# Padding each row of values, keys and output gates from 968 to 1024 words

## The chip, the cores and the metric

The kernel runs on one core of a Trainium2 chip. The metric is device time in microseconds of one execution of the whole program; of several runs the median is taken. All arithmetic is in float32 unless a line says otherwise.

## The reference, cut to what matters

Two layers stand behind each other. The first is a gated recurrence over 768 steps, for 4 batches and 8 heads of width 40:

```python
for t in range(S):
    m_new = np.maximum(f_gate[:, :, t] + m, i_gate[:, :, t])
    f_stab = np.exp(f_gate[:, :, t] + m - m_new)
    i_stab = np.exp(i_gate[:, :, t] - m_new)
    m = m_new
    C = f_stab[..., None, None] * C + i_stab[..., None, None] * np.einsum('bhd,bhe->bhde', vt, kt)
    n = f_stab[..., None] * n + i_stab[..., None] * kt
    h_tilde = np.einsum('bhde,bhe->bhd', C, qt)
    denom = np.maximum(np.abs(np.einsum('bhd,bhd->bh', n, qt)[..., None]), 1.0)
    y[:, :, t] = h_tilde / denom / (1.0 + np.exp(-o_gate[:, :, t]))
```

The second routes each of the 3072 resulting rows (320 wide) to one of 4 groups and in it to one of 4 experts; the chosen expert of 16 computes `relu(x @ w1) @ w2` with 1024 hidden units, and the two gate probabilities scale the row.

## The kernel before, in words

The recurrence is computed in chunks of 128 steps. There are 6 chunks by 4 batches, so 24 units, each with all 8 heads; unit u is chunk u // 4 of batch u % 4. `unit(u)` issues the work of a unit, written out by hand so that neighbouring units overlap: loads for units ahead, scores of unit u + 1, results of unit u, the last scaling and the store of unit u - 1. For the instruction order nothing is planned by the compiler; each engine runs its list as written.

A unit needs three inputs and leaves one output, all moved by DMAs that SyncE (SP) issues on one queue:

- `qk`: keys and queries, transposed, in two DMAs of 40 partitions each, one row of 1024 words to a partition (`load_qk`, lines 157 and 158).
- `nt`: for each of 128 steps a row with 328 words of values (each head's 40 and a one), 320 words of keys and 320 words of output gates, 968 words in all (`load_nt`, line 183). The source is a DRAM array that the host lays out as 24 blocks of 128 rows without gaps. Four tiles take turns.
- `ab`: the decays of the unit's 8 heads, one row of 1024 words that is sent to all 128 partitions (`load_ab`, line 173).
- `x_d`: the unit's 128 result rows of 384 words, stored to DRAM (`store_rows`, line 315), from where the second layer gathers them. In four units a block of 128 rows of zeros is stored too (line 459).

So the queue of SP carries, per unit, in this order: `ab`, `qk`, `qk`, `nt`, `x_d`. Each DMA has one of eight landing counters in turn, and an issue waits until the DMA eight places ahead of it has landed; SP is therefore never more than eight DMAs ahead.

Readers of an `nt` tile are `gate` (ScalarE, tanh of the 320 gate words), `keyw` (GpSimd, keys times decay), `state` and `values` (TensorE, with the values as the moving operand), and `gated` (VectorE, gates times results):

```python
o = st_[u]["nt"][:, NTW:NTW + DM]                      # gate, line 162
t["nt"][:, DM + H:NTW]                                 # keyw, line 220
mm(..., t["kw"][:, j, :], nt[:, j * D1:(j + 1) * D1])  # state, line 257
```

They address words 0 to 967 of a row. `NTW` is 648, the words ahead of the gates.

After the units come the routing, the lists of rows for each expert, and the experts themselves in order of their load; they use neither `nt` nor its array, but their tiles reuse the memory of the units.

Of the kernel before, what the change touches and what calls it, by code (L numbers as in the profile page):

```python
# [7 lines left out]
F32 = mybir.dt.float32  # L8
# [10 lines left out]
P = 128  # L19
B, H, S, D = 4, 8, 768, 40  # L20
NCH = S // P
NU = NCH * B
DM = H * D
# [12 lines left out]
D2 = 2 * D1  # L36
WIN = 64
NTW = 2 * DM + H
CW = 56
NQK = 4  # L40
C_ID, C_LT, C_TIE, C_E, C_P, C_CAP, C_FIRST, C_15E, C_BASE, C_RANK, C_END = (
# [23 lines left out]
def bc(ap, shape):  # L65
    return ap.broadcast_to(list(shape))
# [3 lines left out]
def lstm_moe(ctx: ExitStack, tc: tile.TileContext, gates, qkT, nat, wcat, w1, w2, cst, out):  # L70
# [41 lines left out]
    def att_pool(name, bufs, stack=att, **kw):  # L112
        return stack.enter_context(tc.tile_pool(name=name, bufs=bufs, side="right", **kw))
# [8 lines left out]
    up_ = att_pool("unit", 1, unit_tiles)  # L122
    qkp = [up_.tile([P, 2, 4, P], F32, name=f"qk{i}") for i in range(NQK)]
    Cflat = up_.tile([P, B * 4 * 2 * CW], F32, name="Cflat")
    Cbd = Cflat.rearrange("p (a r e) -> p a r e", r=2, e=CW)[:, :, :, 0:D1]
    abs_ = [up_.tile([P, H, P], F32, name=f"ab{i}") for i in range(4)]
    nts = [up_.tile([P, NTW + DM], F32, name=f"nt{i}") for i in range(4)]
    ps_s = att_pool("ps_s", 3, score_banks, space=PSUM)
    ps_a = att.enter_context(tc.tile_pool(name="ps_a", bufs=1, space=PSUM))
    sums = ps_a.tile([P, 512], F32, name="st")[:, 0:8 * D1].rearrange("p (a r e) -> p a r e", r=2, e=D1)  # L130
# [30 lines left out]
    def gate(u):  # L161
        o = st_[u]["nt"][:, NTW:NTW + DM]
        nc.scalar.activation(o, o, AF.Tanh, scale=0.5)
# [51 lines left out]
    def keyw(u):  # L215
        t = st_[u]
        if u // B < NCH - 1:
            kw = wk.tile([P, H, D], F32, name="kw")
            nc.gpsimd.tensor_tensor(kw.rearrange("p (a r) d -> p a r d", r=2),
                                    t["nt"][:, DM + H:NTW].rearrange("p (a r d) -> p a r d", r=2, d=D),  # L220
                                    bc(t["ab"][:, :, P - 1:].rearrange("p (r a) t -> p a r t", r=2), (P, 4, 2, D)), op=ALU.mult)
# [8 lines left out]
    def carried(u):  # L230
        c, b = divmod(u, B)
        t = st_[u]
        if c > 0:
            acc = acc_of(u)
            for pr in range(4):
                o = (b * 4 + pr) * 2 * CW
                for r in HALVES:
                    mm(acc[r, 2 * pr:2 * pr + 2, 0:D1], t["qk"][:, 1, pr, r],
                       Cflat[:, o:o + 2 * CW].rearrange("p (r e) -> p r e", r=2)[:, :, 0:D1], start=(pr == 0), stop=False,
                       skip_group_check=True)  # L240
# [58 lines left out]
    def gated(u):  # L299
        c, b = divmod(u, B)  # L300
        sr = st_[u]["sr"] = wk.tile([P, H, D], F32, name="sr")
        nc.vector.scalar_tensor_tensor(sr, st_[u]["nt"][:, NTW:NTW + DM].rearrange("p (h d) -> p h d", d=D), 1.0, st_[u]["acc"][:, :, 0:D],
                                       op0=ALU.add, op1=ALU.mult)
# [876 lines left out]
    with tc.manual_schedule():  # L1180
# [131 lines left out]
        for r in range(NEARLY, NE):  # L1312
# [8 lines left out]
            if r + 1 < NE:  # L1321
                first, second = casts(r + 1)
                ahead, k = (1, 1) if CAPS[r] <= P else (1, 2) if CAPS[r] == P + SHORT else (0, 2) if CAPS[r] <= 224 else (0, 4)
# [70 lines left out]
def _lay(inputs):  # L1394
    import numpy as np

    c = np.ascontiguousarray
    q, k, v, o = (inputs[n] for n in ('q', 'k', 'v', 'o_gate'))
    parity = np.r_[0:H:2, 1:H:2]
    gates = c(np.stack([inputs[n][:, parity].reshape(B * H, S) for n in ('f_gate', 'i_gate')], axis=1))  # L1400

    def tr(a):
        return a.reshape(B, H // 2, 2, NCH, P, D).transpose(3, 0, 2, 5, 1, 4).reshape(NCH, B, 2 * D, H // 2, P)

    qkT = c(np.stack([tr(k), tr(q)], axis=3))

    def rows(a):
        return a.reshape(B, H, NCH, P, D).transpose(2, 0, 3, 1, 4)

    vv = np.concatenate([rows(v), np.ones((NCH, B, P, H, 1), v.dtype)], axis=-1)  # L1410
    nat = c(np.concatenate([vv.reshape(NCH, B, P, DM + H)] + [rows(a).reshape(NCH, B, P, DM) for a in (k, o)], axis=-1))
    wg, we = inputs['moe_w_group'], inputs['moe_w_expert']
    wcat = np.concatenate([wg, we.transpose(1, 0, 2).reshape(DM, NE)], axis=1)
    wcat = np.concatenate([wcat, np.zeros((DM, 12), wcat.dtype)], axis=1)
    wcat = np.concatenate([wcat, wcat[2 * P:]], axis=0)
    wcat = c(wcat.reshape(3, P, 32).transpose(1, 0, 2))
    w1 = inputs['moe_w1'].reshape(NE, DM, F)
    w1 = np.concatenate([w1, w1[:, 2 * P:]], axis=1)
    w1 = c(w1.reshape(NE, 3, P, F).transpose(0, 2, 1, 3).reshape(NE, P, 3 * F))
    w2 = c(inputs['moe_w2'].reshape(NE, NF, P, DM).transpose(0, 2, 1, 3).reshape(NE, P, NF * DM))  # L1420
    cst = np.zeros((P, C_END), np.float32)
    cst[:, C_ID:C_ID + P] = np.eye(P)
    cst[:, C_LT:C_LT + P] = np.triu(np.ones((P, P)), 1)
    cst[:, C_TIE:C_TIE + 4] = [4, 3, 2, 1]
    cst[:, C_E:C_E + NE] = np.arange(NE)
    cst[:, C_P] = np.arange(P)
    cst[:, C_CAP:C_CAP + NE] = CAPS
    cst[:, C_RANK:C_RANK + NE] = RANKS
    cst[:, C_FIRST:C_FIRST + NE] = NE - np.arange(NE)
    cst[:, C_15E:C_15E + NE] = NE - 1 - np.arange(NE)  # L1430
    cst[0, C_BASE:C_BASE + NE] = np.arange(NE) * NTOK
    cst[1, C_BASE:C_BASE + NE] = -MID
    return {'gates': gates, 'qkT': qkT, 'nat': nat, 'wcat': wcat, 'w1': w1, 'w2': w2, 'cst': cst}
# [22 lines left out]
```

## Time and profile before

| | |
|---|---|
| median of 3 runs | 381.36 us (378.76, 381.36, 382.41) |
| profiled execution, its own time | 378.54 us |
| its span, first to last instruction | 377.0 us |
| granted clock of TensorE, mean over the span | 0.992 of full speed |
| busy share of the span: TensorE, VectorE, ScalarE, GpSimd | 93%, 78%, 70%, 42% |
| moved by all DMA queues | 89.19 MB, 237 GB/s over the span |

The profile is of one execution. 1.5 us of its time lie outside the span. A DMA is cut into packets, which 16 DMA engines work off; the profile gives for each queue the number of its packets, the bytes, and the time of its packets as a share of 16 engines' time in the stretch. A share over 100% says that packets overlapped or that some ran on past the end of the stretch. Mean time of a packet is that share, times 16, times the length of the stretch, over the number of packets that began in it.

### The profile page before, as it was taken

The numbers are of one execution on the slowest core, as the hardware profiler recorded it, in microseconds if no ns is written. First come the engines' busy times: TensorE is split into PE (matmuls) and PEld (weight loads), VectorE is DVE, ScalarE is ACT, GpSimd is POOL, SyncE is SP. The second block draws the span as 40 slices with busy tenths as digits, with TensorE's granted clock in tenths as the row PEclk, the third lists the DMA queues.
The fourth block names the chain that finished last, engine by engine and source line by source line (L and its number), as shares of the span: only waits on it lengthen the run. The fifth ranks groups of instructions, "written<-read, shape, count | busy, mean of one in ns | idle before, by whom it ended". The sixth has DMA issues, their size and how long they took to land.

```text
span 377.0 us, 10237 instructions
## 1 busy us (share of the span) xinstructions
PE 350.5 (93%) x3809; PEld 310.4 (82%) x3809; DVE 295.6 (78%) x716; ACT 264.0 (70%) x656; POOL 157.2 (42%) x180
## 2 busy tenths in 40 slices
PE   8979989899989769999999989999999999999993
PEld 5747778787777658789999989979989989979993
DVE  5896786778887764588897887898887888889892
ACT  3579777778676454445785875885886788789691
POOL 6586867576745100616322433234322604332131
PEclk9999999999999989999999999999999999999998
DMA  6999999899999790449764866748669759569000
GB/s 187 296 318 323 325 310 323 290 343 343 334 320 316 261 308 5 115 138 343 240 248 158 304 226 198 258 134 285 233 232 285 239 182 314 175 205 287 28 20 15
DMA packets 23572, 89.19 MB, mean 237 GB/s; under 512 B 3904, under 2 KB 7910, under 8 KB 19938
## 3 DMA queue, kind: packets, MB, share of 16 engines
q1 hardware_dynamic: 19442, 76.28, 60.3%
q0 software_dynamic: 3760, 11.87, 10.2%
q8 instruction: 31, 0.51, 0.6%
q10 hardware_dynamic: 320, 0.38, 0.4%
q14 instruction: 19, 0.16, 0.1%
HBM read 78.97 MB, written 10.03 MB: 236 GB/s over the span
## 4 chain that ended last, share of the span: by engine, by line
PE 59%; DMA 16%; issue 9%; DVE 7%; ACT 4%; POOL 3%; POOLq 1%; SPq 0%; DVEq 0%; ACTq 0%
PE psh L770 22%; DMA qk<-in_qkT_dram 10%; DMA x_d<-x 6%; PE po L841 5%; PE po L842 5%; PE po L843 5%; PE po L698 3%; PE sp L207 3%; PE po L814 2%; PE acc L283 2%; ACT ab L198 2%; PE psh L795 2%; DVE w1l L741 1%; PE busy L139 1%; PE lg L350 1%
## 5 line engine op out<-in xcount | busy, mean ns | idle before, releaser
L595 POOL DMA_INDIRECT out_dram<-y,ix x32 | 39.3, 1228 | 105.5 <-ACT y L855 56.5
L770 PE MATMUL psh<-xhl,w1h 128*128 128x256 f32 (+4 forms) x336 | 58.1, 303 | 1.1 <-issue 0.6
L198 ACT ACTIVATE ab<-ab,bcol 128x128 f32<-128x128 f32 x176 | 53.9, 389 | 4.4 <-POOL ab L166 3.8
L841 PE MATMUL po<-w2h,hh 128*128 128x320 f32 (+1 forms) x176 | 55.7, 317 | 0.0
L843 PE MATMUL po<-w2h,hh 128*128 128x320 f32 (+1 forms) x176 | 54.3, 309 | 0.0
L842 PE MATMUL po<-w2l,hh 128*128 128x320 f32 (+1 forms) x176 | 54.3, 309 | 0.0
L770 PEld LDWEIGHTS psh<-xhl,w1h 128*128 128x128 f32 x336 | 49.4, 188 | 3.1 <-issue 1.6
L741 DVE TENSOR_TENSOR w2l<-w2s,w2h 128x640 fp32r<-128x640 f32 x60 | 47.9, 823 | 4.6 <-ACT w2h L737 4.0
L770 PE MATMUL psh<-xhl,wsk 128*128 128x256 f32 (+4 forms) x168 | 47.6, 322 | 0.0
L770 PE MATMUL psh<-xhl,w1l 128*128 128x128 f32 (+6 forms) x256 | 47.5, 267 | 0.0
L591 POOL DMA_INDIRECT xg<-x_d,ix x32 | 32.5, 1017 | 33.9 <-issue 16.5
L741 DVE TENSOR_TENSOR w1l<-w1s,w1h 128x1024 fp32r<-128x1024 f32 x32 | 39.1, 1223 | 7.0 <-ACT w1h L737 6.6
L770 PEld LDWEIGHTS psh<-xhl,w1l 128*128 128x128 f32 x256 | 42.1, 188 | 0.4
L737 ACT CAST w2h<-w2s 128x640 fp32r<-128x640 f32 x60 | 41.7, 724 | 0.1
L207 PE MATMUL sp<-qk 64*128 64x128 f32 x384 | 34.5, 287 | 6.2 <-DMA qk<-in_qkT_dram 4.0
L166 POOL TENSOR_SCALAR_AFFINE_SELECT ab<-ab 128x1024 f32<-128x1024 f32 (+1 forms) x26 | 27.4, 1054 | 26.8 <-DMA ab<-a_d 21.9
L207 PEld LDWEIGHTS sp<-qk 64*128 64x128 f32 x384 | 27.9, 187 | 12.0 <-DVE den L297 3.8
L841 PEld LDWEIGHTS po<-w2h,hh 128*128 128x128 f32 (+1 forms) x176 | 32.6, 185 | 3.4 <-issue 3.1
L212 DVE TENSOR_TENSOR pt<-sp,ab 128x512 f32<-128x512 f32 x48 | 32.0, 683 | 4.1 <-PE sp L207 3.1
L737 ACT CAST w1h<-w1s 128x1024 fp32r<-128x1024 f32 x32 | 33.3, 1044 | 0.0
L843 PEld LDWEIGHTS po<-w2h,hh 128*128 128x128 f32 (+1 forms) x176 | 32.6, 185 | 0.2 <-DVE hh L897 0.2
L842 PEld LDWEIGHTS po<-w2l,hh 128*128 128x128 f32 (+1 forms) x176 | 32.6, 185 | 0.0
(203 smaller groups left out, 738.6 us busy)
## 6 DMA issues: line engine op xcount, KB each, us to landing
w2s<-in_w_dram SPq DMA_DIRECT2D x14, 1280.0 KB
w1s<-in_w_dram SPq DMA_DIRECT2D x12, 1024.0 KB
nt<-in_nat_dram SPq DMA_DIRECT2D x24, 484.0 KB
ab<-a_d SPq DMA_DIRECT2D x22, 512.0 KB
qk<-in_qkT_dram SPq DMA_DIRECT2D x48, 160.0 KB
x_d<-x SPq DMA_DIRECT2D x24, 192.0 KB
w1s<-in_w_dram SPq DMA_DIRECT2D x14, 256.0 KB
w2s<-in_w_dram SPq DMA_DIRECT2D x4, 640.0 KB
```

What stands on the lines that cost most here:

```text
L166: nc.gpsimd.affine_select(out=a, in_=a, pattern=[[0, a.shape[1]], [1, P]], compare_op=ALU.is_ge, fill=fill, base=0, channel_multiplier=-1)
L198: nc.scalar.activation(ab[:, j, :], ab[:, j, :], AF.Exp, bias=bcol[:, c, b * H + j:b * H + j + 1])
L207: mm(t["pm"][hh][:, pr, :], qk[r, 0, pr, :], qk[r, 1, pr, :], start=True, stop=True)
L212: nc.vector.tensor_tensor(pt, t["pm"][hh], t["ab"][:, 4 * hh:4 * hh + 4, :], op=ALU.mult)
L591: return nc.gpsimd.indirect_dma_start(out=o, out_offset=None, in_=src, in_offset=bass.IndirectOffsetOnAxis(ap=idx, axis=0))
L595: return nc.gpsimd.indirect_dma_start(out=out, out_offset=bass.IndirectOffsetOnAxis(ap=idx, axis=0), in_=y, in_offset=None, bounds_check=N ...
L737: nc.scalar.copy(t[names[0]][rows, dst], src[r][rows, s])
L741: nc.vector.tensor_tensor(o, src[r][rows, s], h.bitcast(F32), op=ALU.subtract)
L770: mm(ps[:, g, 0:n_], w[:, s], x, start=(part == 0 and n == 0), stop=(part == 1 and n == len(todo[1]) - 1), skip_group_check=True)
L841: mm(po[0:m], hh[:, f, t], w2h[:, s], start=st0, stop=False)
L842: mm(po[0:m], hh[:, f, t], w2l[:, s], start=False, stop=False)
L843: mm(po[0:m], hh[:, f, tl], w2h[:, s], start=False, stop=sp0)
```

## The change

Each row of 968 words is followed by 56 words of zeros, in the DRAM array and in the four tiles. The rows are laid out on the host, outside the measured time. The one DMA that fills a tile moves whole rows, so it carries the zeros too: 512 KB in place of 484 KB. Nothing reads the added words.

```diff
 NTW = 2 * DM + H
+NTR = 1024
...
-    nts = [up_.tile([P, NTW + DM], F32, name=f"nt{i}") for i in range(4)]
+    nts = [up_.tile([P, NTR], F32, name=f"nt{i}") for i in range(4)]
...
-    nat = c(np.concatenate([vv.reshape(NCH, B, P, DM + H)] + [rows(a).reshape(NCH, B, P, DM) for a in (k, o)], axis=-1))
+    nat = np.concatenate([vv.reshape(NCH, B, P, DM + H)] + [rows(a).reshape(NCH, B, P, DM) for a in (k, o)], axis=-1)
+    nat = c(np.concatenate([nat, np.zeros(nat.shape[:3] + (NTR - NTW - DM,), nat.dtype)], axis=-1))
```

`load_nt` is the same line, `nc.sync.dma_start(nt, nat[c, b])`; line numbers after the new constant are one higher. Every engine's list of instructions, with what each waits for, is the same as before but for the shape of these 24 DMAs. A row now begins at a multiple of 4096 bytes in its block where it began at a multiple of 3872. In the on-chip memory the units' tiles lie at the top end of a stack, so those below the four `nt` tiles (`qk`, `ab`, the state) begin 896 bytes lower, and the four `nt` tiles, 4096 bytes apart now, all begin at the same place modulo 256 bytes, where they had four different ones.

## Rows read from the trace of the kernel before

**Rows 1.** Page, part 2: DMA engines in 40 slices of the span, 9.4 us each.

```profile
DMA  6999999899999790449764866748669759569000
```

**Rows 2.** Chain that ended last, 30 to 125 us: shares by line, then two pieces.

```profile
by line: DMA qk<-in_qkT_dram 41.4%; DMA x_d<-x 22.0%; PE sp L207 9.0%; PE acc L283 7.1%; PE acc L238 3.8%; issue 2.9%; PE lg L350 2.9%; PE tp L325 2.0%; DVE pt L212 1.6%; PE tp L489 1.3%; PE st L257 1.1%; PE lg L356 0.8%; POOL x L307 0.8%; 
...
33.67 7.14 DMA qk<-in_qkT_dram
...
104.09 8.54 DMA qk<-in_qkT_dram
```

**Rows 3.** Waits of SP's queue, 33.7 to 112.7 us: total, times, longest.

```profile
SPq L183 <- DMA ab<-a_d: 12.2, 11, 1.7
SPq L157 <- DMA nt<-in_nat_dram: 4.6, 7, 1.4
```

**Rows 4.** Timeline of SP, one unit: start, length, issue.

```profile
45.46 0.35 SPq L183 DMA_DIRECT2D nt<-in_nat_dram  x1
46.13 0.40 SPq L315 DMA_DIRECT2D x_d<-x  x1
47.27 0.33 SPq L173 DMA_DIRECT2D ab<-a_d  x1
47.96 0.31 SPq L157 DMA_DIRECT2D qk<-in_qkT_dram  x1
...
49.96 0.35 SPq L183 DMA_DIRECT2D nt<-in_nat_dram  x1
```

**Rows 5.** Window 33.7 to 112.7 us: busy time of PE, PEld, DVE, ACT, POOL; clock; DMA.

```profile
33.70:112.70 79.00, 71.47 (x1434) 60.46 (x1430) 60.80 (x219) 59.41 (x212) 53.86 (x75) 1.00 0.99 324
```

**Rows 6.** DMA view, 33.7 to 112.7 us: packets, SP's queue, issues with KB each.

```profile
DMA packets 9056, 25.56 MB, mean 324 GB/s; under 512 B 1149, under 2 KB 3702, under 8 KB 9039
...
q1 hardware_dynamic: 9039, 25.33, 97.5%
...
nt<-in_nat_dram SPq DMA_DIRECT2D x16, 484.0 KB
ab<-a_d SPq DMA_DIRECT2D x15, 512.0 KB
qk<-in_qkT_dram SPq DMA_DIRECT2D x32, 160.0 KB
x_d<-x SPq DMA_DIRECT2D x16, 192.0 KB
x_d<-w1s SPq DMA_DIRECT2D x4, 192.0 KB
```

**Rows 7.** DMA view, 7.1 to 7.3 us.

```profile
DMA packets 14, 0.05 MB, mean 271 GB/s; under 512 B 0, under 2 KB 0, under 8 KB 14
...
q1 hardware_dynamic: 14, 0.05, 67.9%
```

**Rows 8.** DMA view, 134.9 to 135.5 us.

```profile
DMA packets 62, 0.25 MB, mean 423 GB/s; under 512 B 0, under 2 KB 0, under 8 KB 62
...
q1 hardware_dynamic: 62, 0.25, 103.1%
```

**Rows 9.** DMA view, 131.7 to 132.1 us.

```profile
DMA packets 96, 0.15 MB, mean 369 GB/s; under 512 B 0, under 2 KB 96, under 8 KB 96
...
q1 hardware_dynamic: 96, 0.15, 102.5%
```

**Rows 10.** DMA view, 182.9 to 183.7 us.

```profile
DMA packets 39, 0.40 MB, mean 499 GB/s; under 512 B 0, under 2 KB 0, under 8 KB 0
...
q1 hardware_dynamic: 39, 0.40, 117.3%
```

**Rows 11.** Tile `nt`, its loads: length of an issue, min/median/max ns, first and last.

```profile
L183 SPq DMA_DIRECT2D nt<-in_nat_dram x24: 351/352/960, 2.8 to 114.9; - x24
```

**Rows 12.** DMA view, 6.3 to 6.5 us.

```profile
DMA packets 15, 0.05 MB, mean 252 GB/s; under 512 B 2, under 2 KB 2, under 8 KB 15
...
q1 hardware_dynamic: 15, 0.05, 110.6%
```

## The prediction

> **What bounds the kernel now.** I first read the page's slices. TensorE is busy nearly throughout, but the DMA engines have a stretch of their own that is full, the slices from about 9 to 122 us, and idle parts only after it [rows 1]. That is the time of the 24 units; the `nt` loads are issued from 2.8 to 114.9 us [rows 11]. The experts behind it cannot feel the change, except that they begin when the units end: what the units lose or gain reaches the end one for one.
>
> Next, the chain that ended last, between 30 and 125 us. Of these 95 us, 41.4% are the wait for a `qk` load and 22.0% for an `x_d` store, together 60.2 us [rows 2]. The pieces are long (7 to 8.5 us each), far longer than a load's own bytes need, because each is a place in a queue. The queue's waits say the same: SP issues an `nt` load and before it has waited 11 times, 12.2 us in all, for an `ab` load to land, and a `qk` load has waited 7 times for an `nt` load [rows 3]. With eight DMAs in flight and five issued per unit, the reader is to see one thing: whichever transfer the chain names, it stands behind all others, `nt` included, and the chain's DMA time grows with the time of the sum.
>
> The windows view settles how full this is. From 33.7 to 112.7 us the DMA engines have a share of 0.99 while TensorE is busy 71.47 of 79.00 us, at a granted clock of 1.00 (the 2.4 GHz level) throughout [rows 5]. So DMA is the bound there, with TensorE 7.5 us behind it. In these 79 us 16 units pass, 4.9 us each; a unit of the timeline has 4.50 us from one `nt` issue to the next [rows 4].
>
> **The change part by part.** Nothing is removed, no wait is added, no step moves on any queue. 24 loads grow from 484 to 512 KB, 28,672 bytes each. The readers address the same words, so no compute instruction changes. An issue costs SP the same: 0.35 us for `nt` with its 968 words, 0.33 us for `ab` with 1024 [rows 4].
>
> *Is a padded row still one packet?* In the stretch, 16 `nt`, 15 `ab`, 32 `qk` and 20 stores [rows 6] make 16 x 128 + 15 x 128 + 32 x 40 + 20 x 128 = 7,808 rows; with the 1,149 packets under 512 bytes that is 8,957, of 9,056 packets counted. If the 4096-byte rows of `ab` and `qk` were cut in two there would be 3,200 more. So a row of 4096 bytes is one packet, and 128 packets per `nt` load stay 128, eight for each of 16 engines in the mean.
>
> *What does a packet cost?* Four short windows in which all packets are of one size give it, undisturbed:
> - 7.1 to 7.3 us: 14 packets, 271 GB/s x 200 ns / 14 = 3,871 bytes each, so `nt` rows; 67.9% x 16 x 200 / 14 = 155.2 ns [rows 7].
> - 134.9 to 135.5 us: 62 packets of 4,094 bytes by the same sum, that is 4096 (a weight load); 159.6 ns [rows 8].
> - 131.7 to 132.1 us: 96 of 1536 bytes, 68.3 ns [rows 9].
> - 182.9 to 183.7 us: 39 of 10240 bytes, 385.0 ns [rows 10].
>
> The last two give a line of (385.0 - 68.3) / 8,704 = 0.0364 ns per byte. A packet is paid by bytes, not by the piece, which excludes a cost of nothing per packet. For 224 bytes more the line says +8.2 ns; the direct comparison of an `nt` row with a 4096-byte row says 159.6 - 155.2 = +4.4 ns, since the `nt` rows stand about 2 ns above the line. These are both ends of the undisturbed price.
>
> The Trainium skill, page "DMA: Bandwidth & Descriptors", section "How a descriptor splits into AXI transactions", has a rule for that difference: reads start at 256-byte boundaries, and a descriptor that starts between two fetches the unused bytes too, in beats of 32 bytes. Rows at a pitch of 3872 start at all eight multiples of 32, and so would cost 121 to 128 beats, 124.5 in the mean, where a padded one costs 128. That is 2.8% more, and the two rows show 4.4 / 155.2 = 2.8%; by bytes alone it would be 5.8%, 9.0 ns. By the rule the sum below would take its lower end, 0.56 us.
>
> *The sum.* In the DMA-bound stretch there are 16 loads, so 16 x 8 = 128 more costly packets on each engine: 128 x 4.4 ns = 0.56 us, or 128 x 8.2 ns = 1.05 us. A third way, by the rate that the crowded queue reaches there: 16 x 28,672 = 459 KB at 25.33 MB / 79 us = 321 GB/s is 1.43 us [rows 6]. Of this, what falls where the chain runs through DMA reaches the end for certain (60.2 us of it, 76% of 79); in the rest the DMA share is nearly as high, so I let it count in full. The other 8 of the 24 loads [rows 11] are issued before 33.7 us, where the chain runs through compute, or after the stretch; their cost is between nothing, while compute covers them, and 8 x 28,672 bytes at the same rate, 0.72 us, if that cover is gone. I take nothing there, and in the stretch the middle between the two undisturbed prices, 0.8 us: the 4096-byte row is the nearest there is to a padded one, but the `nt` row is of 14 packets only. So +0.8 us, with ends at 0.4 (76% of 0.56) and 2.15 (1.43 + 0.72).
>
> Against the profiled execution that is 378.5 + 0.8 = 379.3 us. That execution was 2.8 us under the median of the runs shown, which themselves spread over 3.7 us; the median moves by the same 0.8 us, to 382.2.
>
> **The rivals.** *Hidden.* The queue has slack that the DMA share doesn't show, and the longer packets only fill it. For it: a unit has 16 engines' share of 0.99, but some of a packet's time is waiting for data, not moving. Then nothing moves: 381.4. Against it: the chain's eight long DMA pieces.
>
> *Faster: the odd starts of the rows are what crowds the engines.* In the stretch the queue's packets took 97.5% x 16 x 79 = 1,232 us of engine time [rows 6]. At undisturbed prices they would take 16 x 128 x 155.2 + 15 x 128 x 159.6 + 32 x 40 x 159.6 + 20 x 128 x 68.3 ns = 1,003 us. So 229 us, 14.3 us per engine, are stretching. If rows that begin at 4096-byte steps ended the `nt` rows' part of it, by their share of the 1,003 us (318, or 32%), that gives back 4.5 us less the 0.8: 377.7. If their odd starts delay the neighbours too, more, down to where TensorE becomes the bound, 7.5 us: 373.9. For it: `nt` is the only load whose rows begin at uneven places. Against it: in a quiet moment its packets take what their bytes ask for, so the unevenness costs 2 ns by itself, and engines that crowd each other explain the rest as well.
>
> *Slower: rows in step.* After the change the rows of all 16 engines begin at the same place modulo 4096 bytes, in DRAM, and their tiles at the same place modulo 256 bytes. If that makes them meet at the same part of a memory, their packets would be stretched as the `nt` packets already are in some moments: from 6.3 to 6.5 us, 13 of them with two tiny ones took 110.6% x 16 x 200 / 13, about 270 ns each [rows 12], 115 ns above the quiet price. At 128 packets per engine that is 14.7 us: 396. The point from which it decides is 3.8 us / 128 = 30 ns per packet. Against it: `qk` rows of 4096 bytes without gaps, and `ab`, one row read 128 times, are in step already, and the stretch carries them at 324 GB/s.
>
> The same page, section "Latency and other measured facts", tells of such a loss where rows lie a large power of two apart: half the rate at 4 MiB, nearly none at 512 KiB. No run here has such a pitch; a padded block is 512 KiB as a whole and its rows are 4 KiB apart, so by that page too this rival is unlikely.
>
> **How the numbers follow.** Forecast, +0.4 to +2.15 us: 0.64. Hidden: 0.20. Faster: 0.08, half of it beyond 1%. Slower: 0.08, nearly all beyond 1%. One per cent, 3.8 us, is about what a measurement of this kernel can tell from no change; forecast and hidden both stay inside it, apart from a few hundredths for the spread of the runs. That makes faster 0.06, same 0.83, slower 0.11. The range takes in forecast and hidden (381.4 to 383.5), about 1.5 us of spread between runs on either side, and the weaker half of the faster rival: 379.0 to 385.2.
>
> **What the profile of the changed kernel would show.** The stretch of full DMA with 16 `nt` loads is 0.4 to 1.5 us longer; MB over the whole span rise by 0.69; the packet count stays; a quiet window with padded rows has about 160 ns per packet; the chain still runs through `qk` and `x_d`, with 55 to 65 us of DMA between 30 and 125 us. Hidden: the same stretch as long as before, at 2% more GB/s. Faster: fewer us of engine time for more bytes, a stretch below 77 us, TensorE's share of it up. Slower: a share of SP's queue over 100% at fewer GB/s, and windows with only padded rows near 200 ns or more. What would make the prediction wrong is an effect of where rows lie, of either sign, above 30 ns per packet; the bytes themselves cannot.

## The result, and the profile after

The changed kernel takes 383.19 us (median of 20 runs, 379.11 to 387.85), the kernel before 380.18 us beside it (20 runs, 374.08 to 383.61): +3.0 us by the medians, 0.8%. The ratio is 1.0124 with an interval of 1.0095 to 1.0153, but it leaves out every run that lies 1.5% above the fastest of its kernel, which for before, with one run of 374.08, is 12 of 20, so the medians are the fairer measure. On another occasion the medians were 382.33 and 379.81, +2.5 us, 0.7%, and the ratio 1.0043 (0.9994 to 1.0091). Resampling the runs gives the two differences of medians an error of 0.7 and 1.1 us. So: slower by 0.7 to 0.8% by the medians; the first comparison excludes no change, the second by itself does not.

The page of the changed kernel, of part 2 the DMA share and the bytes over the span, of part 3 SP's queue:

```profile
DMA  7889999999999972257884786659668768558000
...
DMA packets 23572, 89.88 MB, mean 236 GB/s; under 512 B 3904, under 2 KB 7910, under 8 KB 19938
...
q1 hardware_dynamic: 19442, 76.97, 60.5%
```

The bytes rose by the 0.69 MB that were forecast (89.19 before), and q1 has as many packets as that of a kernel with narrow rows (19,442, below): a padded row is still one packet. The full stretch reaches a slice further than in [rows 1].

The experts cannot be where the time went: from the last `x_d` store of the units to the end it is 242.6 us before and 240.8 after. Over all profiles of the two kernels and of the two with 968-word loads and a wider pitch or tile, told of below, this part takes 240.3 to 242.6 us, while the last store is issued at 134.4 to 136.5 us in the four with narrow rows and at 140.1 and 137.6 in the two of the changed kernel. What is longer lies ahead. I take as the stretch the time from the 8th `nt` issue to the 24th, 16 loads. In before these are at 35.37 and 114.85, after at 36.97 and 117.92 us. The windows view of before for this stretch (busy time of TensorE, its weight loads PEld, VectorE, ScalarE, GpSimd, then clock, DMA share, GB/s):

```profile
35.40:114.90 79.50, 72.05 (x1438) 61.18 (x1440) 61.99 (x223) 59.91 (x214) 54.98 (x77) 1.00 0.99 325
```

The same of after:

```profile
37.00:117.90 80.90, 72.20 (x1438) 61.19 (x1434) 62.14 (x225) 59.96 (x214) 55.24 (x77) 1.00 0.98 322
```

The DMA view of after, same stretch, SP's queue and the `nt` loads:

```profile
q1 hardware_dynamic: 9041, 25.84, 96.4%
...
nt<-in_nat_dram SPq DMA_DIRECT2D x16, 512.0 KB
```

The reader is to see that the rate has not risen (325 to 322 GB/s) while TensorE does the same work (72.05 and 72.20 us): the extra bytes are paid in time. The stretch is 1.5 us longer and begins 1.6 us later. Another 2.6 us of this pair lie between the 24th `nt` issue and the last store, 19.6 us before and 22.2 after; but the second profile of the changed kernel has 19.4 there, and the others with narrow rows up to 21.7, so this part is not the change's. The windows view of that second profile:

```profile
37.00:118.20 81.20, 73.89 (x1464) 62.39 (x1460) 62.42 (x226) 60.54 (x216) 55.14 (x77) 1.00 0.98 323
```

Over all profiles the stretch is 79.49, 78.82, 78.09, 80.24 and 79.70 us with narrow rows in it (mean 79.3) and 80.95, 81.15 and 79.92 with 1024-word rows (mean 80.7): +1.4 us, with an error of 0.5 by their spread. The 8th issue comes at 35.9 us in the mean where the first seven loads are narrow (five profiles, 35.37 to 36.66) and at 36.6 where they are wide (four, 36.21 to 37.02): +0.7, error 0.3, where the narrow ones alone spread over 1.3.

The chain of after, 30 to 125 us, answers to [rows 2]:

```profile
by line: DMA qk<-in_qkT_dram 25.8%; DMA x_d<-x 15.8%; PE sp L208 8.0%; DMA ab<-a_d 7.8%; PE acc L284 7.6%; issue 5.0%; PE acc L239 4.3%; ACT ab L199 2.3%; PE tp L326 2.2%; PE tp L490 1.8%; PE st L258 1.5%; POOL xg L592 1.3%; DVE sr L303 1.3
...
37.64 7.84 DMA x_d<-x
45.49 8.54 DMA qk<-in_qkT_dram
...
79.32 7.45 DMA ab<-a_d
86.78 7.53 DMA qk<-in_qkT_dram
```

Long places in the queue again, with `ab` as a third name. The DMA view of after in a quiet window, 7.4 to 7.6 us, where the second `nt` load lands, as in [rows 7]:

```profile
DMA packets 14, 0.06 MB, mean 287 GB/s; under 512 B 0, under 2 KB 0, under 8 KB 14
...
q1 hardware_dynamic: 14, 0.06, 71.5%
```

That is 71.5% x 16 x 200 / 14 = 163.4 ns per packet, 8.2 above the 155.2 of before: the upper of the two undisturbed prices. By the rule of the Trainium skill, page "DMA: Bandwidth & Descriptors", section "How a descriptor splits into AXI transactions", it would by estimate be 2.8% more; this window shows 5.3%. Since 4096-byte rows of other loads took 159.6 ns [rows 8], 14 packets don't decide it. Loads by themselves, further below, show 2.3% and 3.3%, near that estimate, but not the reason that the rule gives: the same 968 words at even starts, by the same estimate 2.8% cheaper than at uneven ones, took 0.7% more in one run and 0.7% less in another.

### The profile page after: what moved, and what is told of

Read it like the earlier page. It is cut to its first block, busy times and chain, and to the rows that moved or that the text cites. A ratio compares the mean times of both kernels' runs of the same rounds, so it can differ in the third digit from the quotient of the medians.

```text
span 380.9 us, 10237 instructions
## 1 busy us (share of the span) xinstructions
PE 352.7 (93%) x3809; PEld 312.5 (82%) x3809; DVE 293.2 (77%) x716; ACT 264.1 (69%) x656; POOL 160.1 (42%) x180
## 2 busy tenths in 40 slices
DMA packets 23572, 89.88 MB, mean 236 GB/s; under 512 B 3904, under 2 KB 7910, under 8 KB 19938
## 3 DMA queue, kind: packets, MB, share of 16 engines
q1 hardware_dynamic: 19442, 76.97, 60.5%
## 4 chain that ended last, share of the span: by engine, by line
PE 49%; DMA 17%; issue 12%; DVE 10%; ACT 5%; POOL 5%; POOLq 1%; ACTq 0%; DVEq 0%; SPq 0%
PE psh L771 19%; DMA qk<-in_qkT_dram 6%; PE po L842 4%; PE po L844 4%; PE po L843 4%; DMA x_d<-x 4%; PE po L699 3%; ACT ab L199 2%; DMA xg<-x_d,ix 2%; PE sp L208 2%; PE po L815 2%; DMA ab<-a_d 2%; PE acc L284 2%; PE psh L796 2%; DVE w1l L742 2%
## 5 line engine op out<-in xcount | busy, mean ns | idle before, releaser
L742 DVE TENSOR_TENSOR w2l<-w2s,w2h 128x640 fp32r<-128x640 f32 x60 | 47.9, 823 | 4.6 <-ACT w2h L738 2.7
L592 POOL DMA_INDIRECT xg<-x_d,ix x32 | 35.5, 1109 | 33.6 <-issue 16.2
```

Of the source, the lines that this page charges most:

```text
L592: return nc.gpsimd.indirect_dma_start(out=o, out_offset=None, in_=src, in_offset=bass.IndirectOffsetOnAxis(ap=idx, axis=0))
L742: nc.vector.tensor_tensor(o, src[r][rows, s], h.bitcast(F32), op=ALU.subtract)
```

## The experiments

**The queue alone, five kinds of rows.** No computing: SP issues only a unit's five DMAs, over and over.

```python
nc.sync.dma_start(abs_[u % 4], <one row of a_d, to 128>)
nc.sync.dma_start(qk[0:D], qkT[c, b, 0:D])
nc.sync.dma_start(qk[64:64 + D], qkT[c, b, D:2 * D])
nc.sync.dma_start(tiles[k][u % 4][:, 0:n], src[c, b, :, 0:n])
nc.sync.dma_start(x_d[u * P:(u + 1) * P, :], x)
```

> No compute: only the units' five DMAs in their order on SP's queue, 24 units at a time, for five forms of the row load, forwards and backwards (A 968 words of rows of 968; B 1024 of 1024; C 968 words of rows of 1024 into a wide tile; D rows of 968 into a wide tile; E 1032 of 1032); behind them each form's 24 loads with nothing between. The output is not computed, zeros are stored. Theory bytes: per unit B is 0.035 to 0.09 us slower than A, C and D equal A, E is B plus at most 0.015 us. Rival place (where padded rows begin costs more than their bytes): C is as slow as B or slower, E is clearly faster than B although longer. Rival clock (TensorE's clock makes the difference, not the queue): B and A differ by no more than 0.09 us per unit, as by bytes, 2.2 us for 24 units.

Per unit, forward and backward turn: 968 words 4.71 and 4.85 us, 1024 words 4.72 and 4.76, 968 at a pitch of 1024 4.74 and 4.91, 968 in a wide tile 5.17 and 4.98, 1032 words 5.17 and 4.98. One kind differs from itself by up to 0.2, more than what was sought. Inconclusive; but a unit in this bare queue takes within some 5% of what it takes in the kernel (79.5 / 16 = 4.97, with four stores of zeros more in it), so the kernel's stretch runs near the queue's own pace.

**The changed kernel once more, its two parts, and wider rows.** The first is unchanged. The second has the padded array and tile, but moves the 968 words alone. The third pads to 1096.

```diff
-        nc.sync.dma_start(nt, nat[c, b])
+        nc.sync.dma_start(nt[:, 0:NTW + DM], nat[c, b, :, 0:NTW + DM])
```
```diff
-NTR = 1024
+NTR = 1096
```

> The changed kernel once more. All theories: 2.3 to 5.0 us slower than before, in the middle 3.7 (the mean of its 20 runs against the 20 of before), so a ratio of 1.006 to 1.013; its profile tells how much the end of the units moves from one execution to the next.

> Rows lie 1024 words apart in DRAM and in the tiles, but only 968 words of each are moved. Theory bytes: as before, ratio 0.997 to 1.003. Rival place: as the changed kernel, ratio 1.006 to 1.013. Rival clock: between them, by how often the clock falls.

> Rows of 1096 words, 128 added where the change adds 56. Theory bytes: 2.3 times what the change costs: by quiet packet prices 1.8 to 3.6 us, by the crowded rate 4.9 us, so a ratio of 1.005 to 1.013; if the 3.7 us of the change are all bytes, 8.5 us, 1.022. Rival place: the rows no longer begin at steps of 4096 bytes, so no more than the bytes' part, at or under the changed kernel. Rival clock: more idle time, more falls, over 1.013.

Measured beside before at 379.81 (29 runs): again 382.33, ratio above; pitch alone 379.85, 1.0006 (0.9967 to 1.0044); 1096 words 382.68, 1.0084 (1.0046 to 1.0122). The windows view of the kernel with the pitch alone:

```profile
36.10:116.40 80.30, 72.09 (x1458) 61.35 (x1454) 61.65 (x226) 60.60 (x215) 55.09 (x77) 1.00 0.98 319
```

Its page, part 3, SP's queue over the whole span:

```profile
q1 hardware_dynamic: 19442, 76.28, 61.3%
```

At 80.2 us the stretch is the longest of the five with narrow rows (78.1 to 80.2), and the bytes are 0.69 MB fewer than after's with as many packets. So where the rows lie costs nothing and gains nothing that could be seen: both rivals of place fall, the faster one and the slower one. What costs is, as far as these runs tell, the words that are moved. 1096 words add 1.57 MB in 24 loads, 2.3 times as much as 1024, and yet the medians are +2.9 and +2.5, each with an error of about 1: not in proportion, as far as such errors let one say. The profiled execution of 1096 took 385.55 us, 2.9 above its median, so its stretch of 85.4 us is no fair measure; the windows view shows it, and a piece of it in which the clock was at the 1.2 GHz level:

```profile
36.20:121.60 85.40, 74.58 (x1460) 63.45 (x1462) 63.47 (x231) 61.57 (x218) 55.27 (x77) 0.97 0.99 315
...
93.40:96.80 3.40, 3.40 (x61) 3.21 (x57) 1.35 (x5) 0.15 (x1) 1.39 (x2) 0.50 0.99 301
```

**Which loads pay.** Only the first 7 loads move 1024 words, or only the others.

```diff
+        w = NTR if u < 7 else NTW + DM
+        nc.sync.dma_start(nt[:, 0:w], nat[c, b, :, 0:w])
```

(`u >= 7` in the second.) Beside them, before itself with a profile, and before with a 1024-word tile alone.

> Rows lie 1024 words apart; the loads of the first seven units move 1024 words of a row, those of the other 17 move 968. Theory start (the cost that was taken as nothing: the first loads delay the first decays): the mask of the first loaded decays starts at 16.4 us as in the changed kernel, not at 15.2, the x store of unit 1 is issued at about 25.7 us, not at 23.7, and of the change's 3 us 1 to 2 us remain, ratio 1.003 to 1.006. Theory stretch (all of it is bytes in the full stretch): 7 of 24 loads, 0 to 0.9 us, ratio 1.000 to 1.003, and the mask starts at 15.2.

> The opposite: 968 words in the first seven units, 1024 in the other 17. Theory start: the first mask at 15.2 us as before, and what remains is the bytes of the full stretch, 0.6 to 1.4 us, ratio 1.001 to 1.004. Theory stretch: nearly all of the change's cost, 2 to 3.5 us, ratio 1.005 to 1.010.

> The kernel before once more, for a second look at its start and its full stretch. All theories: 376 to 383 us; the first mask at 15.2 us and the stretch from the eighth to the last row load within 1.5 us of the first profile, if the start is as regular as the theory has it.

> The tiles alone are 1024 words wide, rows in DRAM and loads as before. All theories: as before, 376 to 383 us, first mask at 15.2 us. If the place of the tiles counts, the start or the stretch looks as in the changed kernel.

Early 380.76, 1.0035 (0.9999 to 1.0071); late 381.73, 1.0089 (1.0055 to 1.0123); before beside them 379.42 (22 runs). One execution each: before 379.48, the wide tile 377.11, so the tile's place shows no cost in that one. By the medians the 7 early loads give +1.3 us (the interval just touches none) and the 17 others +2.3. The sum, 3.6, is no less than the whole loss. That the early loads, which I had priced at nothing, cost something is likely by this, but not shown.

A theory of my own fell here. In the first profile of after the units begin over 1 us late: GpSimd's first mask of loaded decays starts at 16.41 us in place of 15.15, and unit 1's store is issued at 25.77 in place of 23.68. I had put this on the wide first loads. But in the early kernel, which has them, the mask starts at 15.78 and the store at 25.01, and in the late kernel, whose first loads are narrow, at 16.65 and 25.98, as late as in after; before itself, once more, has 15.66 and 24.93. So a late start comes without wide first loads, and an earlier one with them, and what the +1.3 us are paid for is open.

**The queue alone, more evenly mixed.** Four kinds in six turns each, then the loads by themselves.

> No compute: the units' five DMAs in their order, 16 units at a time, for four forms of the row load in six turns of changing order (A 968 words of rows of 968; B 1024 of 1024; C 968 of rows of 1024; E 1096 of 1096); behind them 16 loads at a time of each form with nothing between, in the same turns. The output is not computed, zeros are stored. Theory bytes at the crowded rate of 321 GB/s: per unit B is 0.09 us and E 0.20 us over A, C equals A; loads alone at the quiet price: B 0.035 to 0.066 us over A per load. Rival busiest engine (the 40-row qk loads keep some engines busier than others, and those set the pace): the same signs, by the quiet packet price alone, B 0.035 to 0.066 and E 0.15 us over A. Rival reaction (the queue doesn't mind, the compute reacts to later landings): B equals A within 0.03 us per unit.

Per unit in the queue, mean of the turns: 968 words 4.87 us (error 0.06), 1024 words 4.76 (0.05), 968 at a pitch of 1024 4.83 (0.05), 1096 words 5.16 (0.09). In the loads by themselves SP issues the first four of a turn at once, and in nearly every turn it then pauses for 4.3 to 5.2 us. A turn of padded rows (start, length, issues):

```profile
1901.61 1.99 SPq L49 DMA_DIRECT2D nb<-in_natp_dram  x4
...
1907.90 14.10 SPq L49 DMA_DIRECT2D nb<-in_natp_dram  x12
```

Two of the 24 turns, one with 968 words and one with 968 at the wide pitch, have no pause, so a mean that takes it in makes narrow rows look cheaper than they are. From the fifth load of a turn to the sixteenth a load takes 1.234 us (0.013), 1.262 (0.010), 1.242 (0.018) and 1.370 (0.014), in the same order; in the first queue run, read the same way, 968 words take 1.216, 1024 words 1.256, 968 at the wide pitch 1.208. So a quiet load pays 0.03 to 0.04 us for 56 words, or 3.5 to 5 ns for each of an engine's eight packets: about the lower of the two undisturbed prices. In the queue 1096 words cost 0.29 us a unit, and 1024 words none.

**Less instead of more.** The gates aren't loaded, so `nt` has 648 words; and, in a second kernel, `qk` loads of 48 rows in place of 40 (8 rows of zeros).

```diff
-        nc.sync.dma_start(nt, nat[c, b])
+        nc.sync.dma_start(nt, nat[c, b, :, 0:NTW])
```
```diff
-        nc.sync.dma_start(qk[0:D], qkT[c, b, 0:D])
-        nc.sync.dma_start(qk[64:64 + D], qkT[c, b, D:2 * D])
+        nc.sync.dma_start(qk[0:48], qkT[c, b, 0:48])
+        nc.sync.dma_start(qk[64:112], qkT[c, b, 48:96])
```

> Before, but the 320 words of output gates are not loaded: ScalarE's tanh and VectorE's product use four tiles of zeros in their place, so every result is half of a gate of zero; all instructions, their sizes and their order stay, each row load moves 648 words. Theory bytes: 3.93 MB less; at 3.1 us per MB that would be 12 us, but TensorE is 7.5 us behind the queue, so 5 to 8 us faster, ratio 0.979 to 0.987, and the DMA share of the stretch well under 0.95. Rival reaction or latency: under 3 us faster.

> Before, but each of the two qk loads of a unit moves 48 partitions, eight of them zeros, in place of 40: 1.57 MB more over the 24 units, 65 KB per unit against the change's 29 KB. Theory bytes at the crowded rate: 4.9 us slower, ratio 1.013. Rival busiest engine: 40 rows cannot be spread evenly over 16 engines, 48 can, three to each; if some engines carry four rows of each load and set the pace, the even spread takes two packets of 160 ns off them per unit, 0.3 us, 5 to 7 us faster in all, ratio 0.981 to 0.987.

Without the gates the kernel took 412.26 us, ratio 1.0866 (1.0808 to 1.0924). I had not reckoned with it: other gates make other `x`, so other tokens for the experts, and an extra pass of a loop that before never enters (TensorE at line 1383, 48 times). The whole time therefore says nothing of the loads. The units' stretch does, in the windows view:

```profile
34.40:105.30 70.90, 67.48 (x1425) 57.93 (x1425) 60.65 (x224) 58.65 (x210) 53.77 (x75) 1.00 0.95 321
```

The group of that extra pass, in the view by line (busy us, mean ns, idle before):

```profile
L1383 PE MATMUL psh<-xhl,w1s 128*128 128x128 f32 (+1 forms) x48 | 15.1, 473 | 0.7 <-DVE xhl L1377 0.7
```

70.9 us for 16 loads instead of 79.5, at the same 321 GB/s: 2.62 MB less are 8.6 us less, 3.3 us per MB, or 305 GB/s (against the mean of the narrow stretches, 79.3, it is 3.2 us per MB). This is the clearest reading of the price of a byte in the full stretch, and it is near the crowded rate (321 in [rows 6]), not the undisturbed one. It is one execution, and of bytes taken out, not added.

The 48-row loads were to be faster by 5 to 7 us if the ten engines that serve a 40-row load were the bound. They are 389.27 us, 1.0259 (1.0202 to 1.0315), 9.5 us slower. Its page, part 2:

```profile
DMA packets 24244, 90.76 MB, mean 233 GB/s; under 512 B 4192, under 2 KB 8198, under 8 KB 20610
```

Its windows view, the stretch and one of three pieces in it at the lower clock:

```profile
37.10:126.80 89.70, 76.84 (x1437) 64.46 (x1439) 61.94 (x224) 59.64 (x212) 55.30 (x77) 0.94 1.04 295
...
38.90:42.30 3.40, 3.40 (x42) 2.37 (x42) 1.69 (x3) 2.10 (x8) 2.95 (x7) 0.51 1.06 280
```

Its DMA view, same stretch:

```profile
q1 hardware_dynamic: 9449, 26.26, 103.0%
```

The page has 4,192 packets under 512 bytes in place of 3,904, so 288 more, six for each of 48 loads. The Trainium skill, page "DMA: Bandwidth & Descriptors", section "Why a DMA increments its semaphore by 16 and not by 1", has it that a DMA runs on the largest number of engines up to 16 that divides its rows, which makes ten for 40 rows and 16 for 48, and that each engine used writes one increment; the six agree. But more engines didn't help. The stretch took 103.0% x 16 x 89.7 = 1,478 us of engine time against some 1,240 before (97.5% of 16 x 79.5 us, the share in [rows 6]); 256 more rows at 159.6 ns are 41 of these 238. The rest is stretched packets, and why they stretch is open. The theory of a busiest engine falls, at least as a way to gain: 4.9 us would have been the price of the added bytes at the crowded rate, and the loss is twice that.

**The queue alone, two kinds in 40 turns.**

> No computing: only the five DMAs of a unit on SP's queue, in the kernel's order, 640 units in 40 turns of 16; the turns use rows of 968 words (n) or padded rows of 1024 words (w), in the order n w w n, ten times over, so that slow drift falls on both alike. Read is the time per unit inside a turn, from one nt issue to the next, the first three of a turn left out. Bytes at the crowded rate: 28,672 bytes at 321 GB/s are +0.09 us per unit for the padded rows. Quiet price: 8 packets by 4.4 to 8.2 ns, +0.035 to +0.066 us. Rival, which the second queue run left standing (4.87 against 4.76 us, each with some 0.05 of spread): rows that fill 4096 bytes make up for their own bytes when nothing else but the queue runs, so 0 or less, down to -0.1 us; then the kernel's loss is not the queue's alone.

Per unit 4.913 us with narrow rows and 4.897 with padded ones (errors 0.036 and 0.053); taken by the ten groups, -0.02 with an error of 0.07. The DMA view of two padded turns, 80.4 to 230.2 us:

```profile
DMA packets 17111, 50.53 MB, mean 337 GB/s; under 512 B 2187, under 2 KB 6330, under 8 KB 17110
...
q1 hardware_dynamic: 17110, 50.52, 96.5%
```

The same of the two narrow turns behind them, 230.2 to 385.7 us:

```profile
DMA packets 17031, 49.45 MB, mean 318 GB/s; under 512 B 2177, under 2 KB 6274, under 8 KB 17030
...
q1 hardware_dynamic: 17030, 49.44, 96.9%
```

The reader is to see 337 GB/s against 318: in these four turns the padded rows ran faster by the byte. Over all 40 the two kinds took the same time, the padded ones for 1.9% more bytes. In the kernel the rate did not rise. Both queue runs together put the price of 56 words at -0.06 us a unit with an error of 0.05, where bytes ask for +0.09 and the kernel's stretches show 1.4 / 16 = +0.09 with an error of 0.03. The bare queue does not reproduce the kernel's loss, so that the loss is the price of bytes in a full queue is not shown by it.

## Why the prediction was right, and where it was mis-sized

**What bounds the kernel: right.** The units' stretch is full of DMA, before and after, TensorE 7 to 9 us behind it. Taking 2.62 MB out of it gave back 8.6 us, until TensorE was 3.4 us behind. The chain still goes through long places in the queue, though `qk`, `x_d` and `ab` together have 49.4% of 95 us, 47 us, and 39.9% in the second profile, and not the 55 to 65 us that I named for DMA. One chain decides little here: with narrow rows these three have from 47.9% to 63.4% in four profiles, and `nt` up to 15.5% beside them.

**The packets: right.** Their number stayed, the bytes rose by 0.69 MB, a quiet one takes 163.4 ns in the one window, and quiet loads pay about the lower price. Of the 3.8 ns between the two prices the prediction gave one reason, the `nt` rows 2 ns above its line; the other half is that the 4096-byte rows stand 2 ns below it.

**The sum: right in sign, too small by about 2 us.** The forecast was +0.8; the two comparisons of medians show +3.0 (error 0.7) and +2.5 (1.1). In the time this shows less, 383.19 against 382.2, by luck of the base: the median of three runs that the forecast was added to, 381.36, stood 1.2 us above that of the 20 runs. The loss itself lies above the forecast's upper end of 2.15. Two terms come into question. *The price of a byte in the stretch:* I took the middle of the undisturbed prices, 0.8 us, and kept the crowded rate only as an upper end, 1.43 us. The stretches show +1.4 (error 0.5), which by itself does not exclude 0.8; the kernel without gates is firmer, 3.3 us per MB, 1.5 for 459 KB. So in this kernel's stretch this term was most likely too small by some 0.6 us. *The loads outside the stretch:* I let compute cover them and took nothing, with 0.72 as an end. The kernel with wide first loads alone shows +1.3, with an interval that touches none, and its start is hardly late; that this term failed is not shown.

**What stays open** is the rest, 1.1 to 1.6 us of the medians beyond the stretch's +1.4, and the law behind it. For bytes alone 1096 words should cost 24 x 65,536 bytes at 321 GB/s, 4.9 us, and its median shows 2.9, which is in the 1.8 to 3.6 us of the undisturbed prices; per wide load, whatever its width, all four kernels would fit: 2.5 to 3.0 and 2.9 for 24 loads, 2.3 for 17, 1.3 for 7, some 0.10 to 0.19 us each. But the bare queue shows nothing for 56 words and 0.29 us for 128. Medians that carry 0.7 to 1.1 us of error don't tell these apart. One part of the excess may be TensorE's clock. In the profiled execution of after it fell to the 1.2 GHz level at 117.1 us, behind a stretch of the chain on VectorE (113.66 to 115.73). The windows view of that piece:

```profile
117.10:120.50 3.40, 3.40 (x52) 3.19 (x49) 2.43 (x8) 1.52 (x6) 1.25 (x2) 0.51 0.99 321
```

The chain of after, the value matmuls before and in it:

```profile
111.96 1.08 PE acc L284 x32
...
116.97 1.74 PE acc L284 x32
```

The same 32 matmuls took 1.74 us in place of 1.08 on the chain. But the second profile of the same kernel has no such fall and the same stretch, and all four profiles with 968-word loads throughout have one of their own near the units' end, beginning between 127 and 139 us. There is another, in the start: where TensorE had to wait longer for the keys (`kw`) at about 21 us, the clock stood at the 1.2 GHz level right behind. The wait in after, its window, and the wait in before, where the granted clock is 1.00 (the 2.4 GHz level) from 20 to 25 us:

```profile
21.22 0.54 PE L258 MATMUL st<-nt,kw 128*40 128x41 f32 x16 [2.46 <-POOL kw L220]
...
21.60:25.00 3.40, 3.40 (x28) 2.27 (x23) 2.03 (x6) 1.83 (x7) 3.40 (x4) 0.50 0.97 350
...
20.05 0.51 PE L257 MATMUL st<-nt,kw 128*40 128x41 f32 x16 [0.96 <-POOL kw L219]
```

Six of nine profiles have this fall, three of four with wide first loads and three of five with narrow ones, and their 8th issue is at 36.4 us in the mean, against 35.9 in the other three. So the +0.7 us of the 8th issue may be this in part. The clock as a cause is argued, not shown.

**The rivals.** Hidden falls: the stretch grew at the same GB/s, and the medians of both comparisons are slower. Faster and slower by the place of the rows both fall by the pitch alone, 1.0006. The stretched `nt` packets of [rows 12] don't come from odd row starts. The DMA view of the kernel with the pitch alone, 6.4 to 6.6 us, where its second `nt` load begins:

```profile
DMA packets 16, 0.05 MB, mean 232 GB/s; under 512 B 4, under 2 KB 4, under 8 KB 16
...
q1 hardware_dynamic: 16, 0.05, 112.5%
```

Here 12 rows with four tiny packets took 112.5% x 16 x 200 / 12, about 300 ns each, at even starts, and not less than the 270 at uneven ones.

## What to carry to other kernels

In a stretch where the DMA engines are full and the chain goes from one place in the queue to the next, price added bytes at the stretch's own rate, here about 3.2 us per MB, rather than at that of a quiet moment, and leave room above it: the whole loss here was about twice that price, for reasons that stayed open. Read loads by themselves only where their issues are paced by landings, not across the pause at the start of a turn. Padding rows to a round length had no worth of its own here: the pitch was neutral to 0.4%, and the zeros were paid like data; if a pitch is wanted, move only the words that are read. And an experiment that changes data which steer later work must be read in the stretch it is about, not in the whole time.

## What the runs showed of the hardware that was not expected

- Loads of 48 rows over more engines, with 4% more bytes in the stretch, made it 13% longer (79.5 to 89.7 us) at 295 GB/s, with a share of 103% for SP's queue; three pieces of 3.4 us at a granted clock of 0.50 or 0.51 (the 1.2 GHz level) lie in it, where before has none.
- Turns of the same DMAs in a bare queue differ by up to some 15%: of the 40 turns of the last run 29 took 4.64 to 4.95 us per unit, and eleven, of both kinds of rows, 5.05 to 5.36.
- Quiet loads of 1024 words took 2.3% and 3.3% longer than loads of 968 words, for 5.8% more bytes (1.234 and 1.262 us, 1.216 and 1.256).
- The place of rows and tiles modulo 4096 or 256 bytes made no difference that these runs can see: 1.0006 (0.9967 to 1.0044).
